# An mLSTM with two feed-forward layers on one core: q-k products in plain fp32 for eighteen more units, and two small TensorE groups joined

## The chip, the cores and the metric

The kernel runs on one core of a Trainium2 chip. The metric is the device time of one execution in microseconds, of which the median of several runs is given. TensorE is written PE, VectorE DVE, ScalarE ACT, GpSimd POOL; SP issues the transfers (DMAs).

## The reference

An mLSTM over 4 batches, 8 heads, 768 steps and head dimension 40 is followed by two feed-forward layers on its 3072 x 320 output. All is in fp32 (the weights arrive as float64).

```python
for t in range(S):                                     # mLSTM, per batch and head
    m_new = maximum(f[t] + m, i[t])
    f_stab, i_stab = exp(f[t] + m - m_new), exp(i[t] - m_new)
    C = f_stab * C + i_stab * outer(v[t], k[t])
    n = f_stab * n + i_stab * k[t]
    y[t] = sigmoid(o_gate[t]) * (C @ q[t]) / maximum(abs(n @ q[t]), 1.0)
x = y as (3072, 320)
x = ((x @ w1) * (x @ w2) @ w3) @ w_out                 # d_ff 1024
out = maximum(maximum(x @ w1b, x @ w2b), x @ w3b) @ w_outb   # d_ff 768
```

## The kernel before

**The mLSTM is done in chunks.** A sequence of 768 steps is cut into eight chunks of 88 and one of 64. A *unit* is one chunk of one batch for four heads; there are 72, and 18 make a batch. Two units (the two head groups) make one chunk of x. For unit u the kernel forms, per head, `s` = the products of 88 keys with 88 queries, `pk` = s times the decay weights `dd` (with the carried state's rows beneath), and `o` = pk against the values and a column of ones, which also yields the state of the next chunk. DVE then updates the state part of `kv` of unit u+2 and divides (four small instructions on `rd`, into `y`), POOL multiplies by the gate, PE transposes y (`xt`), and ACT and DVE split the transposed x into two parts, `xh` (rounded to the reduced form fp32r) and `xl` (the rest).

**How s is formed.** For the first `NP` = 10 units it is a plain fp32 matmul of 40 rows from tile `raw` (line 565). From unit 10 on q and k are split too: the load brings copies of q and k on 120 partitions, ACT rounds them into `qs` (line 571) and `kst` (573), POOL subtracts for qs (575) and DVE for kst (579), and one fp32r matmul over 120 rows adds the three products (line 586). The o matmuls (line 606) are fp32 throughout.

**The layers are done in token blocks of 384**, eight of them, in pairs: block A of two token blocks, then block C of the two. A group (lines 678 to 682) is eight fp32r matmuls of 384 columns into a `wk` bank. Block A has 8 steps of two groups (the product of x@w1 and x@w2); its result, split by ACT (`ph`) and POOL or DVE (`pl`), goes against w3@w_out (lines 745 to 749), a product that the kernel forms itself from fp32 matmuls, the *folds* (line 906). Block C has 6 steps of three groups (the maximum), and lines 764 for w_outb. Weights arrive as float64 and are turned into fp32 by ACT and DVE in *granules* (lines 833 to 856), then split into two parts (`wah`/`wal`, `wch`/`wcl`, 866 and 869) or stacked (`war`, `wcr`, 881 and 888).

**What sets the order.** No engine's order is written by hand. The program notes every operation with its engine, a duration in ns, and what it reads and writes; `Plan.run` then plays the whole program with these durations, with latencies between engines (`LAT`), with a clock for PE and a bus for the DMAs (`XFER`), and gives a free engine the ready operation with the least latest start, shifted by a table of biases by engine and tile (`BIAS`). The order so found is the order in which the engines' instructions are issued. `USTEPS` and `UNEXT` say behind which steps of a pair of token blocks a new unit is begun. Both s and o use the two `aq` banks of PSUM.

Of the kernel before, what the change touches and what calls it, by code (L numbers as in the profile page):

```python
# [8 lines left out]
F32 = mybir.dt.float32  # L9
# [16 lines left out]
NG = 3 * NC  # L26
NU = B * NCH * 2
GL = [L] * 8 + [64]
NP = 10
FOLDS = (3,6,9)  # L30
XLAG = 1
NPR = 7
# [6 lines left out]
L_BUFS = 4  # L39
RCP = 8  # L40
RAW0 = 3
LAST = (NBLK - 1, 1, NC - 1)
LATE = ("A", 1, 4)
BUF = dict(x=3, y=3, og=4, ph=2, ev=3, raw=2, kv=3, vs=3, qq=2, dd=4, qs=2, pk=2, rd=5)
LAT = dict(
    PA=200, PV=200, AV=130, AG=160, GA=90, GV=90, VA=130, VG=155, VP=200, AP=200, GP=230, DA=-50, DV=-50, DG=-30, DP=-50,
    VD=150, GD=150, AD=150,
)
AHEAD = 2500
GRAB = dict(V=140, G=177)  # L50
XFER = 1.45
BIAS = {"Add": -32750, "Aev": 31250, "Ag": -210500, "Akst": -383000, "Aph": -77500, "Aqs": -262250,
        "Asa": -13500, "Asg": 43250, "Astg": 57250, "Asx": 232000, "Awa": 7750, "Awar": -174000,
        "Awb": -221500, "Awc": 71000, "Awcr": -19750, "Awd": -55000, "Axh": -124000, "Dcs": -138250,
        "Ddd": 34000, "Ddna": 62500, "Dev": 75000, "Dg": -534000, "Dkv": 54250, "Dkvb": -129250, "Dqq": -96500,
        "Draw": 58250, "Dsg": -183000, "Dstg": 57750, "Dsx": -234500, "Dvs": 56750, "Gdd": 194250,
        "Gg": 144250, "Gmp": -23000, "Gpk": -77750, "Gpl": 36250, "Gqqb": -55750, "Gqs": -400500,
        "Gvsb": 10500, "Gwa": 379750, "Gwar": 219500, "Gwc": 102000, "Gwcr": 176500, "Gwd": 49000,
        "Gy": -128500, "Pac0": 27250, "Pac1": -309750, "Pac2": -91000, "Po": 7500, "Ppt": -14000, "Ps": -61250,
        "Pwk": 14250, "Pxt": -39750, "S-": -110000, "Sg": -305500, "Vam": -30000, "Vev": 474750, "Vg": -54250,  # L60
        "Vkst": 81500, "Vkv": -147750, "Vmp": -268500, "Vpk": -108500, "Vsa": -44000, "Vsg": 32250,
        "Vstg": 104500, "Vsx": -56500, "Vwb": -108500, "Vxl": 80250, "Vy": -35250, "Vzero": -14500}
TICK = 10240 / 3
WARM = 0
BANKS = ("wk", "aq", "ac0", "ac1", "ac2")
STOP = ("A", 0, 4)
U0 = (1, 1, 1, 1, 1, 1, 1, 1)
USTEPS = (8, 9, 11, 12, 15, 16, 20, 21, 23, 25, 27)
UNEXT = (0, 1, 2, 3, 4, 6, 7)


# [206 lines left out]
def mlstm_moe_kernel(  # L278
# [78 lines left out]
    def new(key, shape, dt, tag):  # L357
        P.tile(key, tag, len(slots[tag]))
        made[key] = view(slots[tag][turn[tag] % len(slots[tag])], shape, dt)
        turn[tag] += 1  # L360
        if gates_done.get(tag):
            P.state[key][0][None] = gates_done[tag]
        return key

    def T(*key):
        return made[key]

    def dma(ns, fn, r=(), w=()):
        return P.op("D", ns, fn, r, w)
# [148 lines left out]
            P.op("V", 69 + 6.25 * DM / RCP, lambda sl=sl: V.reciprocal(out=T(*t)[:, sl], in_=T(*t)[:, sl]), w=[t])  # L518

    def unit(u):  # L520
        load(u + 2)
        b, c, g, n, r = ub(u)
        h0 = b * 8 + g * 4
        if u < NP:
            new(("raw", u), [48, 4, 2 * L], F32, "raw0")
            dma(333, lambda: SP.dma_start(out=T("raw", u), in_=qk0[g, c]), w=[("raw", u)])
        else:
            new(("raw", u), [120, 2, 4, L], F32, "raw")
            dma(888, lambda: SP.dma_start(out=T("raw", u), in_=qk[b, g, c]), w=[("raw", u)])
# [30 lines left out]
        if u < NP:  # L560

            def f():
                raw = T("raw", u)
                for h in range(4):
                    PE.matmul(T("s", u)[:L, h], lhsT=raw[0:40, h, L:2 * L], rhs=raw[0:40, h, 0:n], start=True, stop=True)

            P.op("P", 720, f, r=[("raw", u)], w=[("s", u)])
        else:
            ks = kst[u % 2]
            new(("qs", u), [120, 4, n], F32R, "qs")  # L570
            P.op("A", act(4 * n), lambda: A.copy(out=T("qs", u), in_=T("raw", u)[:, 0, :, 0:n]),  # L571
                 r=[("raw", u)], w=[("qs", u)])
            P.op("A", act(4 * n), lambda: A.copy(out=ks, in_=T("raw", u)[:, 1]),
                 r=[("raw", u)], w=[("kst", u % 2, 1)])
            P.op("G", 889, lambda: G.tensor_tensor(  # L575
                out=T("qs", u)[0:40], in0=T("raw", u)[0:40, 0, :, 0:n], in1=T("qs", u)[0:40].bitcast(F32),
                op=ALU.subtract,
            ), r=[("raw", u)], w=[("qs", u)])
            P.op("V", dve(4 * n), lambda: V.tensor_tensor(
                out=ks[64:104], in0=T("raw", u)[64:104, 1], in1=ks[64:104].bitcast(F32),  # L580
                op=ALU.subtract,
            ), r=[("raw", u)], w=[("kst", u % 2, 1)], port=1)

            def f():
                for h in range(4):
                    PE.matmul(T("s", u)[0:L, h], lhsT=ks[:, h], rhs=T("qs", u)[:, h], start=True, stop=True)  # L586

            P.op("P", 390, f, cols=90, r=[("qs", u), ("kst", u % 2)], w=[("s", u)])
        if L < r:

            def scaled(e):
# [7 lines left out]
        if u < 10:
            new(("o", u), [128, 4, 41], F32, f"ac{u % 3}")  # L600
        else:
            new(("o", u), [128, 4, 41], F32, "aq")

        def f():
            for h in range(4):
                PE.matmul(T("o", u)[:m, h], lhsT=T("pk", u)[:r, h, 0:m], rhs=T("kv", u)[:r, h, 40:81],  # L606
                          start=True, stop=True)

        P.op("P", 910 if m > n else 500, f, cols=210, r=[("pk", u), ("kv", u)], w=[("o", u)])
        if m > n:  # L610
            P.op("V", dve(164), lambda: V.scalar_tensor_tensor(
                out=T("kv", u + 2)[64:128, :, 40:81], in0=T("o", u)[64:128], scalar=cs[64:128, 168:169],
                in1=T("vs", u + 2)[64:128], op0=ALU.mult, op1=ALU.add,
            ), r=[("o", u), ("kv", u + 2, "k"), ("vs", u + 2)], w=[("kv", u + 2, "s")])
# [308 lines left out]
    def late_w(q):  # L923
# [13 lines left out]
            return ()  # L937
        before = switch[-1:]
        if q == 1:
            assert cur[0] >= NP and folds[0] == NA  # L940
            for key, (_, _, acc) in P.state.items():
                if key[0] in ("raw", "sg", "w3", "wo", "sx", "mp"):
                    before += acc
# [19 lines left out]
    def more():  # L963
        u = cur[0]
        if u < NU:
            unit(u)
            if u % 2:
                pend.append(ub(u)[:2])
            cur[0] = u + 1

    folds = [0]
# [75 lines left out]
def _lay(i):  # L1047
# [77 lines left out]
```

## Time and profile before

| what | value |
| --- | --- |
| three runs | 732.37, 736.55, 738.3 us; median 736.55 |
| the profiled execution | 735.73 us |
| its span, first to last instruction | 733.9 us |
| busy: PE, DVE, ACT, POOL | 695.5, 453.4, 385.7, 337.2 us |
| mean granted clock of PE | 0.988 |
| moved by DMA | 82.48 MB |

Busy times add up the instructions of an engine; several engines work at once, so they don't add up to the span. An engine's instructions run in their order; an instruction that waits holds up those behind it. The ends of matmuls are modelled, so the distance between the starts of two matmuls is a better measure of what one costs than its own length.

### The profile page before, as it was taken

The numbers are of one execution on the slowest core, as the hardware profiler recorded it, in microseconds if no ns is written. First come the engines' busy times: TensorE is split into PE (matmuls) and PEld (weight loads), VectorE is DVE, ScalarE is ACT, GpSimd is POOL, SyncE is SP. The second block draws the span as 40 slices with busy tenths as digits, with TensorE's granted clock in tenths as the row PEclk, the third lists the DMA queues.
The fourth block names the chain that finished last, engine by engine and source line by source line (L and its number), as shares of the span: only waits on it lengthen the run. The fifth ranks groups of instructions, "written<-read, shape, count | busy, mean of one in ns | idle before, by whom it ended". The sixth has DMA issues, their size and how long they took to land.

```text
span 733.9 us, 12690 instructions
## 1 busy us (share of the span) xinstructions
PE 695.5 (95%) x4269; PEld 670.2 (91%) x4269; DVE 453.4 (62%) x1012; ACT 385.7 (53%) x728; POOL 337.2 (46%) x465
## 2 busy tenths in 40 slices
PE   1797899999999999999999999999999999999998
PEld 1675887788999999999999999999999999999998
DVE  4679998878775668475454777564454774232433
ACT  5978989888884336545334345554342342232211
POOL 1859875857744345565423555564243461000000
PEclk9999999999999999999999999999999999999999
DMA  8998777955623335433212446332222340000000
GB/s 211 251 268 244 226 217 236 239 153 161 190 88 87 102 82 148 130 92 87 75 30 70 114 102 169 94 101 80 57 68 64 92 108 1 1 0 1 1 28 27
DMA packets 52232, 82.48 MB, mean 112 GB/s; under 512 B 11864, under 2 KB 37912, under 8 KB 52168
## 3 DMA queue, kind: packets, MB, share of 16 engines
q1 hardware_dynamic: 52168, 81.69, 40.3%
q8 instruction: 33, 0.54, 0.3%
q14 instruction: 31, 0.25, 0.1%
HBM read 77.63 MB, written 4.03 MB: 111 GB/s over the span
## 4 chain that ended last, share of the span: by engine, by line
PE 78%; DMA 7%; DVE 4%; ACT 4%; POOL 3%; issue 2%; SPq 0%; POOLq 0%; DVEq 0%; ACTq 0%
PE wk L678 12%; PE wk L680 12%; PE wk L679 12%; PE ac L764 8%; PE aq L606 6%; PE wk L682 6%; PE wk L681 6%; PE ac L745 4%; PE ac L749 4%; DMA dd<-d_na 4%; PE ac L747 3%; PE aq L586 2%; PE wk L906 1%; PE aq L646 1%; ACT stg L850 1%
## 5 line engine op out<-in xcount | busy, mean ns | idle before, releaser
L698 POOL TENSOR_TENSOR pl<-pr,ph 128x384 fp32r<-128x384 f32 (+1 forms) x30 | 31.2, 1040 | 161.1 <-ACT ph L694 141.9
L694 ACT CAST ph<-pr 128x384 fp32r<-128x384 f32 (+1 forms) x114 | 57.4, 507 | 86.3 <-PE ac L764 38.3
L678 PE MATMUL wk<-xh,wch 128*128 128x384 f32 x288 | 99.6, 346 | 0.2 <-ACT pr L726 0.2
L729 DVE TENSOR_TENSOR pr<-pr,wk 128x384 f32<-128x384 f32 (+1 forms) x98 | 53.2, 545 | 71.0 <-PE wk L682 67.9
L680 PE MATMUL wk<-xl,wch 128*128 128x384 f32 x288 | 97.1, 337 | 0.0
L679 PE MATMUL wk<-xh,wcl 128*128 128x384 f32 x288 | 97.0, 337 | 0.0
L698 DVE TENSOR_TENSOR pl<-pr,ph 128x384 fp32r<-128x384 f32 (+1 forms) x84 | 53.6, 638 | 67.3 <-ACT ph L694 66.5
L678 PE MATMUL wk<-xh,wah 128*128 128x384 f32 x256 | 91.7, 358 | 1.6 <-ACT xh L657 1.6
L680 PE MATMUL wk<-xl,wah 128*128 128x384 f32 x256 | 87.5, 342 | 2.8 <-DVE xl L660 2.8
L679 PE MATMUL wk<-xh,wal 128*128 128x384 f32 x256 | 87.4, 342 | 0.8 <-DVE wal L869 0.8
L575 POOL TENSOR_TENSOR qs<-misc,qs 40x352 fp32r<-40x352 f32 (+1 forms) x62 | 66.4, 1072 | 39.8 <-ACT qs L571 37.9
L541 POOL TENSOR_TENSOR dd<-am,dd 128x352 f32<-128x352 f32 (+2 forms) x72 | 59.9, 831 | 53.8 <-DMA dd<-d_na 49.1
L726 ACT COPY pr<-wk 128x384 f32<-128x384 f32 x48 | 23.2, 484 | 89.8 <-PE wk L682 89.8
L632 POOL TENSOR_TENSOR misc<-misc 88x160 f32<-88x160 f32 (+1 forms) x62 | 42.6, 687 | 54.5 <-DVE misc L627 54.2
L711 ACT COPY pr<-wk 128x384 f32<-128x384 f32 x64 | 31.0, 484 | 68.6 <-PE wk L682 68.6
L606 PEld LDWEIGHTS aq<-kv,pk 128*128 128x128 f32 (+2 forms) x496 | 59.3, 184 | 5.0 <-issue 2.2
L713 DVE TENSOR_TENSOR pr<-pr,wk 128x384 f32<-128x384 f32 x64 | 35.4, 553 | 41.7 <-PE wk L682 40.7
L606 PE MATMUL aq<-kv,pk 128*128 128x41 f32 (+2 forms) x496 | 58.9, 268 | 1.7 <-DVE misc L627 1.4
L850 ACT ACTIVATE stg<-stg 128x512 f16<-128x512 f32 (+2 forms) x41 | 52.2, 1281 | 7.4 <-DVE stg L842 6.7
L549 ACT ACTIVATE dd<-dd 128x352 f32<-128x352 f32 (+2 forms) x72 | 35.2, 490 | 39.9 <-POOL dd L545 36.0
L678 PEld LDWEIGHTS wk<-xh,wch 128*128 128x128 f32 x288 | 54.2, 188 | 0.5 <-ACT pr L726 0.5
L679 PEld LDWEIGHTS wk<-xh,wcl 128*128 128x128 f32 x288 | 54.2, 188 | 0.0
(130 smaller groups left out, 1755.7 us busy)
## 6 DMA issues: line engine op xcount, KB each, us to landing
misc<-in_qk SPq DMA_DIRECT2D x62, 330.0 KB
dd<-d_na SPq DMA_DIRECT2D x56, 176.0 KB
kv<-in_kv SPq DMA_DIRECT2D x72, 121.5 KB
stg<-in_w3t SPq DMA_DIRECT2D x13, 512.0 KB
stg<-in_wc SPq DMA_DIRECT2D x9, 512.0 KB
qq<-in_qk SPq DMA_DIRECT2D x64, 66.0 KB
misc<-in_og SPq DMA_DIRECT2D x31, 120.0 KB
out<-misc SPq DMA_DIRECT2D x23, 160.0 KB
```

The source lines that it names most:

```text
L541: P.op("G", 735, lambda: G.tensor_tensor(out=T("dd", u)[:r], in0=am[:r, c, h0:h0 + 4].unsqueeze(2).to_broadcast([r, 4, n]), in1=T("dd", u) ...
L575: P.op("G", 889, lambda: G.tensor_tensor(out=T("qs", u)[0:40], in0=T("raw", u)[0:40, 0, :, 0:n], in1=T("qs", u)[0:40].bitcast(F32), op=ALU ...
L606: PE.matmul(T("o", u)[:m, h], lhsT=T("pk", u)[:r, h, 0:m], rhs=T("kv", u)[:r, h, 40:81], start=True, stop=True)
L678: PE.matmul(p, lhsT=h_[:, kt], rhs=xh[:, kt], start=kt == 0, stop=False)
L679: PE.matmul(p, lhsT=l_[:, kt], rhs=xh[:, kt], start=False, stop=False)
L680: PE.matmul(p, lhsT=h_[:, kt], rhs=xl[:, kt], start=False, stop=False)
L681: PE.matmul(p, lhsT=r_, rhs=xh[:, 2], start=False, stop=False)
L694: P.op("A", act(n), lambda sl=sl: A.copy(out=T("ph", key)[:, sl], in_=T(*src)[:, sl]), r=[src + part], w=[("ph", key) + part])
L698: e.tensor_tensor(out=T("pl", key)[:, sl], in0=T(*src)[:, sl], in1=T("ph", key)[:, sl].bitcast(F32), op=ALU.subtract)
L729: P.op("V", dve(sl.stop - sl.start), lambda ps=ps, sl=sl: V.tensor_tensor(out=T(*sc)[:, sl], in0=T(*sc)[:, sl], in1=T(*ps)[:, sl], op=ALU. ...
L764: PE.matmul(T(f"ac{m}", (k, 1)), lhsT=src[:, m * 128:m * 128 + 128], rhs=w[:, o:o + DM], start=first_, stop=last_,)
L850: A.activation(out=sign, in_=tl()[:, :, 1].bitcast(F32), func=AF.Copy)
```

## The change

Three things. `NP` goes from 10 to 28, so that units 10 to 27 form s by the plain fp32 matmul from a load of 48 partitions as well (`qk0` now holds all batches); `NQ` = 10 keeps the first ten in their own buffers. From unit `DUO` = 28 on, s of unit u and o of unit u-1 are one operation to the planner (1210 ns in place of 390 and 910), issued back to back; the loads of unit u+2 are noted after o of unit u-1, what followed an o before (the state's update, y, the gate) is now the function `rest`, and a chunk becomes due for its transpose when its y is done. The planner's latencies from ACT to DVE and to POOL go from 130 to 165 and from 160 to 210 ns, `XFER` from 1.45 to 1.5, one more step (26) begins a unit, and the table of biases is another.

```diff
-NP = 10
+NP = 28
+NQ = 10
+DUO = 28
-    PA=200, PV=200, AV=130, AG=160, GA=90, ...
+    PA=200, PV=200, AV=165, AG=210, GA=90, ...
-XFER = 1.45
+XFER = 1.5
-BIAS = {"Add": -32750, "Aev": 31250, "Ag": -210500, "Akst": -383000, "Aph": -77500, "Aqs": -262250,
+BIAS = {"Add": -25500, "Aev": 67500, "Ag": -141500, "Akst": -365750, "Aph": -135500, "Aqs": -321000,
...
-USTEPS = (8, 9, 11, 12, 15, 16, 20, 21, 23, 25, 27)
+USTEPS = (8, 9, 11, 12, 15, 16, 20, 21, 23, 25, 26, 27)
...
     def unit(u):
-        load(u + 2)
+        if u < DUO:
+            load(u + 2)
...
         if u < NP:
-            new(("raw", u), [48, 4, 2 * L], F32, "raw0")
-            dma(333, lambda: SP.dma_start(out=T("raw", u), in_=qk0[g, c]), w=[("raw", u)])
+            new(("raw", u), [48, 4, 2 * L], F32, "raw0" if u < NQ else "raw")
+            dma(333, lambda: SP.dma_start(out=T("raw", u), in_=qk0[b, g, c]), w=[("raw", u)])
...
+            duo = u >= DUO
+            if duo:
+                new(("o", u - 1), [128, 4, 41], F32, "aq")
+
             def f():
                 for h in range(4):
                     PE.matmul(T("s", u)[0:L, h], lhsT=ks[:, h], rhs=T("qs", u)[:, h], start=True, stop=True)
-
-            P.op("P", 390, f, cols=90, r=[("qs", u), ("kst", u % 2)], w=[("s", u)])
+                if duo:
+                    outs(u - 1)
+
+            if duo:
+                P.op("P", 1210, f, cols=300, r=[("qs", u), ("kst", u % 2), ("pk", u - 1), ("kv", u - 1)],
+                     w=[("s", u), ("o", u - 1)])
+            else:
+                P.op("P", 390, f, cols=90, r=[("qs", u), ("kst", u % 2)], w=[("s", u)])
...
-        P.op("P", 910 if m > n else 500, f, cols=210, r=[("pk", u), ("kv", u)], w=[("o", u)])
+        if u >= DUO:
+            rest(u - 1)
+            load(u + 2)
+        if u + 1 < DUO or u == NU - 1:
+            new(("o", u), [128, 4, 41], F32, f"ac{u % 3}" if u < 10 else "aq")
+            P.op("P", 910 if m > n else 500, lambda: outs(u), cols=210, r=[("pk", u), ("kv", u)], w=[("o", u)])
+            rest(u)
+
+    def outs(u):
+        b, c, g, n, r = ub(u)
+        m = 128 if c < NCH - 1 else n
+        for h in range(4):
+            PE.matmul(T("o", u)[:m, h], lhsT=T("pk", u)[:r, h, 0:m], rhs=T("kv", u)[:r, h, 40:81], start=True, stop=True)
+
+    def rest(u):
...
```

In the order of the changed program the lines are about 20 higher: 565 becomes 569, 586 becomes 594, 606 becomes 625, 646 becomes 666, 678 to 682 become 698 to 702, 694 becomes 714, 711 becomes 731.

The first place is ACT in the first block A, between the second and the third eviction of a `wk` bank (`COPY pr<-wk`). Before:

```order
L711 COPY pr_115<-wk_131 128x384
L833 ACTIVATE stg_111<-stg_111 128x512
L839 ACTIVATE sx_121<-sx_121 128x512
L866 CAST wah<-stg_113 128x512
L850 ACTIVATE stg_111<-stg_111 128x512
L573 CAST kst_74<-misc 120x352
L573 CAST kst_75<-misc 120x352
L571 CAST qs_94<-misc 120x352
L571 CAST qs_95<-misc 120x352
L694 CAST ph_87<-pr_115 128x384
L711 COPY pr_116<-wk_130 128x384
```

And now:

```order
L731 COPY pr_115<-wk_131 128x384
L870 ACTIVATE stg_111<-stg_111 128x512
L859 ACTIVATE sx_121<-sx_121 128x512
L714 CAST ph_87<-pr_115 128x384
L853 ACTIVATE sx_121<-sx_121 128x512
L886 CAST wah<-stg_111 128x512
L731 COPY pr_116<-wk_130 128x384
```

The four casts of q and k of two units are gone, and the granules of weights have moved up by one.

The second place is PE in the same block, around its third group. Before, an s, the group, and then another s with an o:

```order
L682 MATMUL wk_130<-xl_83,war 128x384
L586 MATMUL aq_133<-qs_94,kst_74 88x88 x4
L678 MATMUL wk_131<-xh_80,wah 128x384
L679 MATMUL wk_131<-xh_80,wal 128x384
L680 MATMUL wk_131<-xl_83,wah 128x384
L678 MATMUL wk_131<-xh_80,wah 128x384
L679 MATMUL wk_131<-xh_80,wal 128x384
L680 MATMUL wk_131<-xl_83,wah 128x384
L681 MATMUL wk_131<-xh_80,war 128x384
L682 MATMUL wk_131<-xl_83,war 128x384
L586 MATMUL aq_133<-qs_95,kst_75 88x88 x4
L606 MATMUL aq_132<-kv_104,pk_96 128x41 x4
```

And now:

```order
L702 MATMUL wk_130<-xl_83,war 128x384
L569 MATMUL aq_133<-misc 88x88 x4
L625 MATMUL aq_132<-kv_104,pk_96 128x41 x4
L698 MATMUL wk_131<-xh_80,wah 128x384
L699 MATMUL wk_131<-xh_80,wal 128x384
```

The s reads the loaded tile itself (`misc` holds raw), it stands ahead of the o, and the first of the two s's has moved to before the first group.

The third place is PE in the block A of token block 2, with the fp32r s of one unit. Before, it stands ahead of a transpose, and the o comes some groups later:

```order
L682 MATMUL wk_131<-xl_83,war 128x384
L586 MATMUL aq_132<-qs_94,kst_74 88x88 x4
L646 MATMUL aq_133<-cs,misc 128x88 x3
L678 MATMUL wk_129<-xh_80,wah 128x384
L679 MATMUL wk_129<-xh_80,wal 128x384
```

And now:

```order
L769 MATMUL ac_135<-pl_88,wb 128x384
L594 MATMUL aq_133<-qs_94,kst_74 88x88 x4
L625 MATMUL aq_132<-kv_104,pk_97 128x41 x4
L698 MATMUL wk_131<-xh_80,wah 128x384
L699 MATMUL wk_131<-xh_80,wal 128x384
```

The s and the o of the unit before it stand together, as in 44 places of the new order (6 before); the transpose stands elsewhere.

## Rows read from the trace of the kernel before

**Rows 1.** The page's slices: PE's busy tenths in 40 equal slices of the span.

```profile
PE   1797899999999999999999999999999999999998
```

**Rows 2.** Busy time by stage: PE, PEld, DVE, ACT, POOL, clock, DMA share, GB/s.

```profile
69.00:136.00 67.00, 58.94 (x333) 52.24 (x334) 59.57 (x117) 60.05 (x104) 49.46 (x58) 0.92 0.81 232
136.00:186.00 50.00, 47.75 (x269) 44.06 (x268) 40.11 (x86) 44.33 (x81) 35.52 (x41) 0.97 0.61 177
186.00:734.00 548.00, 543.20 (x3439) 536.31 (x3438) 306.27 (x705) 228.01 (x469) 211.37 (x297) 1.00 0.28 76
```

**Rows 3.** PE's waits from 69 to 186 us: us in total, times, longest.

```profile
PE wk L680 <- DVE xl L660: 2.8, 1, 2.8
PE aq L646 <- POOL misc L632: 1.8, 3, 0.8
PE wk L678 <- ACT xh L657: 1.6, 1, 1.6
PE aq L606 <- DVE misc L627: 1.4, 1, 1.4
PE aq L586 <- POOL pk L555: 1.1, 1, 1.1
PE wk L679 <- DVE wal L869: 0.8, 1, 0.8
PE wk L906 <- ACT qs L571: 0.6, 1, 0.6
PE aq L586 <- DVE misc L627: 0.6, 1, 0.6
```

**Rows 4.** Busy time of the three stretches at half clock, columns as in rows 2.

```profile
69.00:76.50 7.50, 4.69 (x15) 4.38 (x16) 7.25 (x11) 6.58 (x14) 7.15 (x8) 0.55 0.84 245
100.00:104.00 4.00, 4.00 (x16) 4.00 (x16) 3.77 (x11) 3.60 (x6) 3.70 (x6) 0.57 0.81 258
168.50:172.00 3.50, 3.50 (x15) 3.40 (x15) 3.10 (x5) 3.06 (x8) 2.26 (x2) 0.54 0.63 200
```

**Rows 5.** Groups by line and shape, 69 to 186 us: busy us, mean ns.

```profile
L575 POOL TENSOR_TENSOR qs<-misc,qs 40x352 fp32r<-40x352 f32 x14 | 16.9, 1213 | 4.5 <-ACT qs L571 2.9 <-PE ac L749 1.4
L579 DVE TENSOR_TENSOR kst<-misc,kst 40x352 fp32r<-40x352 f32 x16 | 14.1, 881 | 0.5
L573 ACT CAST kst<-misc 120x352 fp32r<-120x352 f32 x16 | 7.9, 503 | 0.7 <-PE aq L586 0.4 <-DMA misc<-in_qk 0.2
L571 ACT CAST qs<-misc 120x352 fp32r<-120x352 f32 x14 | 6.7, 484 | 0.0
```

**Rows 6.** PE's timeline: an fp32r s alone (start us, us).

```profile
76.86 0.44 PE L586 MATMUL aq<-qs,kst 120*88 120x88 f32 x4
77.12 0.42 PE L678 MATMUL wk<-xh,wah 128*128 128x384 f32 x1
77.39 0.34 PE L679 MATMUL wk<-xh,wal 128*128 128x384 f32 x1
77.56 0.34 PE L680 MATMUL wk<-xl,wah 128*128 128x384 f32 x1
```

**Rows 7.** PE's timeline: an fp32 s in the start-up.

```profile
57.28 0.85 PE L565 MATMUL aq<-raw 40*88 40x88 f32 x8
58.06 0.45 PE L646 MATMUL aq<-cs,misc 88*128 88x88 f32 x3
```

**Rows 8.** DMA issues of q and k from unit 10 on.

```profile
misc<-in_qk SPq DMA_DIRECT2D x62, 330.0 KB
```

**Rows 9.** PE's timeline: an o alone.

```profile
270.70 0.98 PE L606 MATMUL aq<-kv,pk 128*128 128x41 f32 x8
271.51 0.42 PE L678 MATMUL wk<-xh,wah 128*128 128x384 f32 x1
```

**Rows 10.** PE's timeline: an o directly after an s.

```profile
280.61 1.06 PE L606 MATMUL aq<-kv,pk 128*128 128x41 f32 x8
281.51 0.69 PE L764 MATMUL ac<-wd,ph 128*128 128x320 f32 x3
```

More of the change, by code (lines that the diff above doesn't have):

```diff
@@ L45 @@
 LAT = dict(
-    PA=200, PV=200, AV=130, AG=160, GA=90, GV=90, VA=130, VG=155, VP=200, AP=200, GP=230, DA=-50, DV=-50, DG=-30, DP=-50,
+    PA=200, PV=200, AV=165, AG=210, GA=90, GV=90, VA=130, VG=155, VP=200, AP=200, GP=230, DA=-50, DV=-50, DG=-30, DP=-50,
     VD=150, GD=150, AD=150,
@@ L50 @@
 GRAB = dict(V=140, G=177)
-XFER = 1.45
-BIAS = {"Add": -32750, "Aev": 31250, "Ag": -210500, "Akst": -383000, "Aph": -77500, "Aqs": -262250,
[L53 to L62, printed above, removed]
+XFER = 1.5
+BIAS = {"Add": -25500, "Aev": 67500, "Ag": -141500, "Akst": -365750, "Aph": -135500, "Aqs": -321000,
+        "Asa": -45750, "Asg": 67750, "Astg": 27000, "Asx": 241250, "Awa": -1750, "Awar": -257250,
+        "Awb": -195750, "Awc": 39750, "Awcr": -11000, "Awd": -9250, "Axh": -135750, "Dcs": -129750,
+        "Ddd": 56500, "Ddna": 63500, "Dev": 137000, "Dg": -506500, "Dkv": 54750, "Dkvb": -159000,
+        "Dqq": -44500, "Draw": 59500, "Dsg": -192750, "Dstg": 60750, "Dsx": -222250, "Dvs": 61500,
+        "Gdd": 191750, "Gg": 141750, "Gmp": -73250, "Gpk": -91000, "Gpl": 83000, "Gqqb": -72500,
+        "Gqs": -332250, "Gvsb": -42250, "Gwa": 408750, "Gwar": 289500, "Gwc": 102250, "Gwcr": 215500,
+        "Gwd": 61500, "Gy": -54000, "Pac0": 20500, "Pac1": -296000, "Pac2": -168000, "Po": -12750,
+        "Ppt": -44000, "Ps": -111500, "Pwk": 5500, "Pxt": -23250, "S-": -146000, "Sg": -268250, "Vam": -34500,
+        "Vev": 394000, "Vg": -91750, "Vkst": 65500, "Vkv": -92000, "Vmp": -289250, "Vpk": -82500,
+        "Vsa": -34250, "Vsg": 48000, "Vstg": 107750, "Vsx": -92500, "Vwb": -169000, "Vxl": 14750, "Vy": -56000,
+        "Vzero": 64250}
 TICK = 10240 / 3
@@ L598, in unit @@
         ), r=[("s", u), ("dd", u)], w=[("pk", u, 1)])
[L599 to L607, printed above, removed]
-        P.op("P", 910 if m > n else 500, f, cols=210, r=[("pk", u), ("kv", u)], w=[("o", u)])
-        if m > n:
+        if u >= DUO:
[11 more added lines that the diff above has]
+    def rest(u):
+        b, c, g, n, r = ub(u)
+        if c < NCH - 1:
             P.op("V", dve(164), lambda: V.scalar_tensor_tensor(
@@ L637, in unit @@
                  r=[("y", (b, c), 1)], w=[("y", (b, c), 2)])
+            pend.append((b, c))
     def x_cols(b, c):
@@ L939, in late_w @@
         if q == 1:
-            assert cur[0] >= NP and folds[0] == NA
+            assert cur[0] >= NQ and folds[0] == NA
             for key, (_, _, acc) in P.state.items():
@@ L966, in more @@
             unit(u)
-            if u % 2:
-                pend.append(ub(u)[:2])
             cur[0] = u + 1
@@ L1055, in _lay @@
     eye = np.eye(D, dtype=f)
-    qk0 = qk[0].transpose(0, 1, 2, 4, 3, 5)
-    qk0 = qk0.reshape(2, NCH, D, 4, 2 * L)
-    qk0 = np.concatenate([qk0, np.zeros((2, NCH, 48 - D, 4, 2 * L), f)], 2)
+    qk0 = qk.transpose(0, 1, 2, 3, 5, 4, 6)
+    qk0 = qk0.reshape(B, 2, NCH, D, 4, 2 * L)
+    qk0 = np.concatenate([qk0, np.zeros((B, 2, NCH, 48 - D, 4, 2 * L), f)], 3)
     qk = np.concatenate([qk, qk[:, :, :, 0:24], qk, qk[:, :, :, 24:40]], 3)
```

## The prediction

> **What bounds the kernel now.** I read the page's slices first. TensorE (PE) is near or over nine tenths busy in all but the first eight or nine of the 40 slices, so the kernel is a start-up followed by a long stretch that is worth exactly its matmul time [rows 1]. Then busy time by stage [rows 2]. Four stages matter: 0 to 69 us, before the first group of block A of token block 0; 69 to 136 us, that block A and the wait for token block 1; 136 to 186 us, block A of token block 1; and 186 us to the end. From 186 us PE is busy 543.20 of 548 us, at full granted clock: nothing is to be had there but fewer or cheaper matmuls, and every matmul added there is added to the end. From 69 to 186 us PE is busy 58.94 of 67 and 47.75 of 50 us, 10.3 us idle, at a mean clock of 0.92 and 0.97, while VectorE (DVE) and ScalarE (ACT) are at 60 of 67 us and GpSimd (POOL) at 49. Nobody is full, and PE waits now for one, now for another. So I asked for PE's waits in that stretch [rows 3] and for the stretches at half clock [rows 4].
>
> The waits fall in two classes. 2.8 and 1.6 us are the very start: the first group wants the two halves of x of token block 0 (xl from DVE, xh from ACT). The others, some 7.5 us as the rows add up, are holes in a running stream: transposes that wait for the gated y from POOL (1.8), an o that waits in a row of DVE work (1.4), an s that waits on POOL's queue (1.1), a weight half that DVE had not yet made (0.8), and five smaller ones. The half-clock stretches are 69 to 76.5, 100 to 104 and 168.5 to 172 us, at means of 0.55, 0.57 and 0.54, that is nearly all at 1.2 GHz, the lower of the two levels; ahead of each PE had been idle for 1 to 3 us. The second and the third cost 4.0 x 0.43 = 1.7 and 3.5 x 0.46 = 1.6 us. So 69 to 186 us holds 7.5 + 3.3 = 10.8 us that less work on DVE, ACT and POOL could give back; the start's 4.4 us and its half-clock matmuls I leave where they are.
>
> **The change part by part.** *s in fp32 for units 10 to 27.* Removed per unit: ACT copies qs (0.484 us) and kst (0.503), DVE subtracts for kst (0.881) and POOL for qs (1.213) [rows 5]. 16 of the 18 units stand between 69 and 186 us, and there these rows alone (two shorter qs left out) are 7.9 + 6.7 = 14.6 us of ACT, 14.1 of DVE and 16.9 of POOL, 14, 14 and 20% of what the engines do in that stretch (104.4, 99.7 and 85.0 us) [rows 2, 5]. None of it is on the path by itself; it is what the waits of rows 3 stand in line behind. The order shows it at its sharpest on ACT: before, four copies stand in a row between a weight's cast and the cast and eviction that block A wants next, 2 us in which ACT does nothing for PE; after, they are gone, though the planner has drawn later weight work and the x of token block 1 into part of the space.
>
> Added on PE per unit: four fp32 matmuls of 88 columns for four fp32r ones. The fp32r s takes 0.26 us from its start to the next group's start, and the first step behind it is longer by 0.1 us, 0.27 where the next is 0.17 [rows 6]. The fp32 s is there only in the start-up: eight records, 0.78 us from its start to the next start at full clock [rows 7]. In those rows it stands between other fp32 matmuls, whose weight loads are longer, so 0.78 is the upper end. The lower end is twice the fp32r one, since there are twice the records: 0.52. I take 0.61, a little over the lower end, because the record count is what the two have in common and the surroundings are not. So +0.26 to +0.52, taken as +0.35, and for 18 units **+6.3 us** (4.7 to 9.4). All of it lies on PE where PE is the bound or close to it, so it counts in full.
>
> The Trainium skill, FP8 and Floating Point Precision, section TensorE Precision Notes, says that true FP32 takes four passes through the array where the reduced form takes one. By that, an estimate from the page and the fp32r row, the s would cost 4 x 0.26 = 1.04 us, +0.78 per unit or +14.0 us in all, and the sum below would be 742. The trace does not agree, since the fp32 s as it stands in rows 7 takes 0.78 us and not 1.04.
>
> The load of raw shrinks from 330 KB a unit [rows 8] to 132 (48 x 704 values of 4 bytes), 3.6 MB in all. PE's waits of 69 to 186 us name no DMA, so this is worth nothing directly; SP issues one DMA for it as before.
>
> *s(u) and o(u-1) joined from unit 28 on.* The planner books 1210 ns for the pair where it booked 390 + 910, a saving of 90 ns in 44 groups. The rows don't show it. Alone, o takes 0.81 us to the next start [rows 9], and s 0.26, and each makes the step behind it 0.09 longer (read behind the s [rows 6], and taken for the o as well): 1.25 us. Directly after an s, o takes 0.90 [rows 10]: 0.26 + 0.90 + 0.09 = 1.25 us. The longer step between two kinds of matmul is only moved from behind the s to between s and o. So **0** us, with -4.0 (the planner's price) and +2.5 as bounds: before, 28 of the 62 fp32r s stood directly ahead of a transpose and shared that step with it, as the order of before shows, and the joined ones can't. What the join adds is a wait: o(u-1) now stands behind s(u), so it waits for qs and kst of unit u as well, and the state's update on DVE (kv of unit u+1), y and the transposes behind it. PE's order covers that: each o comes some six to twelve matmul groups earlier than before after 186 us, because a unit more is begun in each pair of blocks, and a unit comes only every few us.
>
> *Latencies and biases.* They cost nothing themselves; they move work. Between the first group and block A of token block 1 PE gets half of its folds fewer (12 of 24 fold matmuls move behind it), so that block A of block 1 can start as soon as its x is there, and the folds fill holes afterwards. For the start at 69 us the order gives no gain that I can price: the bytes ahead of the first weights are the same to within 0.2 MB, and DVE has as much work ahead of the last xl of token block 0 as before. I take 0, with 2 us either way. From 620 us on no unit is left and nothing changes.
>
> *The sum.* The profiled execution took 735.73 us (span 733.9), 0.8 below the median of the three runs, 736.55. Added +6.3. Given back: of the 10.8 us, the wait of s on POOL (1.1) and the later one of s behind DVE (0.6) go for certain, as nothing is left to wait for; of the other 9.1 I take two thirds, 6.1, because 14 to 20% of the work in front of them goes but part of the space is filled again. So 735.73 + 6.3 - 7.8 = 734.2, rounded to **734 us**, 0.3% under the median: no difference that a measurement of this kernel tells from none (about 1%, as its three runs lie 732.37 to 738.3).
>
> **The rivals.** *All holes go* (faster): the whole 10.8 comes back, the fp32 s costs its lower end, and the start is 2 us earlier: 735.7 + 4.7 - 10.8 - 2 = 728. For it: three engines lose a seventh to a fifth of their work at once, and a half-clock stretch vanishes with the hole ahead of it. Against it: DVE and ACT do as much work up to the end of the first block A as before, since later work moves up.
>
> *PE pays and the holes stay* (slower than before): one mechanism, in block A of token blocks 0 and 1. If the planner refills ACT and DVE so far that PE still waits for a weight half, a pk or a y, only the two s waits go (1.7), and at the upper price of fp32 the time is 735.7 + 9.4 - 1.7 = 743; at the price I took, 740. It decides from the point where less than 6.3 us of the 15 us of idle and half-clock time between the first group and 186 us are given back. For it: PE's own work between the first group and the first block C grows by some 6 us, to over nine tenths of that stretch.
>
> *The join pays after all*: if the planner's 90 ns are real, -4.0 us and 730. Against it stand rows 9 and 10. *The join makes PE wait*: s(u) held for POOL's qs now holds o(u-1) too; at 0.2 us for each of 44 groups, 743. Against it: in 186 us to the end PE's waits are almost nil today. *The fp32 s costs four times the fp32r one* among fp32r groups: 4 x 0.26 is 0.78 more for each of 18 units [rows 6], 735.7 + 14.0 - 7.8 = 742; rows 7 speak against it. This is the result that the page named above would give.
>
> **How the numbers follow.** Forecast 0.55; all holes go 0.17; holes stay 0.15; join pays 0.07; join waits 0.04; four times 0.02. The forecast's own bounds are some 5 us either way, from the price of fp32 (4.7 to 9.4) and the share given back. The range takes in the first two rivals: 727 to 745. Faster by over 1% is below 729.2: most of the first rival, a third of "join pays" and a tenth or more of the forecast, 0.25. Slower by over 1% is above 743.9: a little under half of the slower rivals and a small tail of the forecast, 0.14. The rest, 0.61, is within 1%.
>
> **What would show it.** In the profile of the changed kernel: the fp32 s among fp32r groups at 0.5 to 0.7 us to the next start (0.78 or more: my price is too low). PE's waits between the first group and the first block C: no s that waits for POOL, some 4 us of holes beside the start's, one half-clock stretch or none after 80 us. The first block C group starts at 184 to 188 us against 186. Joined groups: o after s at 0.90 us; 0.81 would mean that the join pays. The first group at 67 to 71 us. From the first block C to the end about 1 us longer than now, for the two units left there. The forecast is wrong if the start moves by more than 2 us, which I could not price, or if the holes of block A neither shrink nor stay but move to the folds that now lie inside it.

## The result, and the profile after

| what | before | after |
| --- | --- | --- |
| median, same chip, 8 runs each | 737.88 us (732.37 to 739.5) | 730.08 us (728.57 to 731.25) |
| ratio after / before | | 0.9913, interval 0.9888 to 0.9937 |
| profiled execution, span | 735.73, 733.9 us | 731.25, 729.3 us |

The change makes the kernel 0.9% faster, by 7.8 us in the medians. The two profiled executions are 4.5 us apart, since that of before lies 2.2 us under its median and that of after 1.2 over; what follows accounts for these 4.5 us, and the other 3.3 are the scatter of single executions.

The page's slices of after (PE's busy tenths in 40 equal slices, to hold against [rows 1]):

```profile
PE   1699999999999999999999999999999999999998
```

The fourth and fifth slices, 55 to 92 us, have filled up: from the third slice on PE is at nine tenths. Busy time by stage (PE, PEld, DVE, ACT, POOL, clock, DMA share, GB/s), the last row being the only stretch at half clock after the first group:

```profile
69.00:136.00 67.00, 63.80 (x401) 56.27 (x401) 51.27 (x124) 60.71 (x92) 44.27 (x62) 0.97 0.76 218
136.00:186.00 50.00, 50.00 (x291) 44.43 (x290) 34.46 (x79) 42.13 (x73) 27.88 (x32) 1.00 0.55 160
186.00:729.30 543.30, 539.29 (x3426) 535.09 (x3424) 303.47 (x693) 220.09 (x458) 196.47 (x279) 1.00 0.27 74
82.00:86.00 4.00, 4.00 (x16) 4.00 (x16) 3.83 (x10) 4.00 (x7) 3.84 (x5) 0.58 0.92 304
```

Against [rows 2], PE gained 4.9 and 2.3 us of busy time in the two block-A stages, and the second stage is full, at full clock. DVE lost 8.3 and 5.7 us, POOL 5.2 and 7.6; ACT lost 2.2 us in the second stage and nothing in the first, where later work has moved up. Of the three half-clock stretches in [rows 4] none stands where it stood; the one left, the last row, follows a wait of 1.4 us for POOL. PE's waits from 69 to 186 us (us in all, times, longest):

```profile
PE aq L625 <- POOL pk L559: 1.4, 1, 1.4
PE aq L569 <- DVE kv L630: 0.8, 1, 0.8
PE aq L569 <- DMA misc<-in_qk: 0.7, 1, 0.7
PE aq L569 <- DVE pk L610: 0.3, 1, 0.3
```

The eight kinds of wait shown in [rows 3], 10.7 us, have become four with 3.2. The s (line 569) now waits once for the transfer of its raw tile, and still twice behind DVE.

To compare kernels whose stages start at different times I cut the span at PE's own milestones: the first group of block A of token block 0, the first group of block C, and the last group. In each stretch the *PE work* is the number of groups of each kind times what such a group takes in the dense stream at full clock, with what it adds to the steps beside it; stretch minus PE work is the *slack*: idle time, half-clock time and steps that come late by less than the profile counts as a wait. The two kernels between these milestones (before, then after; columns as above):

```profile
68.90:186.10 117.20, 106.78 (x602) 96.40 (x602) 99.79 (x201) 104.58 (x184) 85.08 (x99) 0.94 0.72 208
186.10:723.60 537.50, 536.13 (x3394) 529.51 (x3394) 302.29 (x694) 226.70 (x465) 210.91 (x296) 1.00 0.28 76
```

```profile
71.60:184.50 112.90, 110.39 (x672) 98.01 (x671) 81.82 (x195) 99.52 (x159) 68.39 (x89) 0.98 0.67 195
184.50:719.00 534.50, 533.83 (x3391) 529.89 (x3390) 300.91 (x685) 219.63 (x457) 197.50 (x279) 1.00 0.28 74
```

| stretch | before | after | difference |
| --- | --- | --- | --- |
| to the first group | 68.9 | 71.6 | +2.7 |
| first group to first block C | 117.2 (work 98.9, slack 18.3) | 112.9 (109.0, 3.9) | -4.3: work +10.1, slack -14.4 |
| first block C to last group | 537.5 (slack 6.2) | 534.4 (2.8) | -3.1: work +0.3, slack -3.4 |
| last group to the end | 10.3 | 10.3 | 0 |

The slack can be read in the rows: from the first group to block C idle time went from 10.4 to 2.5 us, and what the lower clock costs from 6.7 us (three stretches, [rows 4]) to 1.7 (4.0 us at 0.58). The later start is no loss: before, the first group began and then stalled for 2.8 us for xl [rows 3]; after, it runs on, and the fourth group starts at 78.3 us against 79.8.

What a small group costs is read from start to start. An fp32 s between groups, a joined pair, and a transpose alone (PE's timeline of after: start, us):

```profile
86.42 0.34 PE L702 MATMUL wk<-xl,war 128*128 128x384 f32 x1
86.69 0.85 PE L569 MATMUL aq<-misc 40*88 40x88 f32 x8
87.47 0.45 PE L698 MATMUL wk<-xh,wah 128*128 128x384 f32 x1
87.76 0.33 PE L699 MATMUL wk<-xh,wal 128*128 128x384 f32 x1
...
300.32 0.39 PE L666 MATMUL aq<-cs,misc 88*128 88x88 f32 x3
300.50 0.42 PE L698 MATMUL wk<-xh,wah 128*128 128x384 f32 x1
300.76 0.34 PE L699 MATMUL wk<-xh,wal 128*128 128x384 f32 x1
...
306.00 0.44 PE L594 MATMUL aq<-qs,kst 120*88 120x88 f32 x4
306.26 1.06 PE L625 MATMUL aq<-kv,pk 128*128 128x41 f32 x8
307.15 0.42 PE L698 MATMUL wk<-xh,wah 128*128 128x384 f32 x1
307.42 0.34 PE L699 MATMUL wk<-xh,wal 128*128 128x384 f32 x1
```

The fp32 s takes 0.78 us to the next start, the step behind it 0.29 and the step ahead of it 0.27, where the dense one is 0.174: it adds 0.27 + 0.78 + 0.29 - 2 x 0.174 = 0.99 to the stream. The longer step ahead is there in all twelve places of after where an fp32 s follows a large fp32r matmul without a wait (0.26 to 0.30). Ahead of an fp32r s the step is 0.17, and the fp32r s of [rows 6] adds 0.53 - 0.174 = 0.35. So one costs **0.64** us more. The expectations below reckon with 0.90 and 0.54, which leave out the step ahead. The joined pair adds 0.26 + 0.89 + 0.27 - 0.174 = 1.25, as much as the two apart (0.35 + 0.89, medians of many). A transpose alone adds 0.18 + 0.26 - 0.174 = 0.27.

### The profile page after: what moved, and what is told of

Its sections match the earlier page's. It is cut to its first block, busy times and chain, and to the rows that moved or that the text cites. A ratio compares the mean times of both kernels' runs of the same rounds, so it can differ in the third digit from the quotient of the medians.

```text
span 729.3 us, 12666 instructions
## 1 busy us (share of the span) xinstructions
PE 699.4 (96%) x4341; PEld 674.3 (92%) x4341; DVE 437.0 (60%) x998; ACT 373.8 (51%) x697; POOL 308.3 (42%) x438
## 4 chain that ended last, share of the span: by engine, by line
PE 84%; DMA 7%; DVE 3%; POOL 2%; issue 2%; SPq 1%; ACT 0%; POOLq 0%; DVEq 0%
PE wk L698 13%; PE wk L699 12%; PE wk L700 12%; PE ac L784 9%; PE aq L625 6%; PE wk L702 6%; PE wk L701 6%; PE ac L765 4%; PE ac L769 4%; PE wk L926 4%; PE ac L767 3%; DMA stg<-in_w3t 2%; PE aq L569 2%; PE aq L594 1%; DMA dd<-d_na 1%
## 5 line engine op out<-in xcount | busy, mean ns | idle before, releaser
L718 DVE TENSOR_TENSOR pl<-pr,ph 128x384 fp32r<-128x384 f32 (+1 forms) x91 | 60.8, 669 | 75.8 <-ACT ph L714 73.1
L718 POOL TENSOR_TENSOR pl<-pr,ph 128x384 fp32r<-128x384 f32 (+1 forms) x23 | 24.2, 1052 | 153.7 <-ACT ph L714 138.9
L545 POOL TENSOR_TENSOR dd<-am,dd 128x352 f32<-128x352 f32 (+2 forms) x72 | 57.5, 799 | 49.6 <-DMA dd<-d_na 48.8
L559 POOL TENSOR_TENSOR pk<-kv,dd 128x160 f32<-128x160 f32 (+1 forms) x64 | 38.7, 606 | 72.1 <-PE aq L625 64.9
L625 PE MATMUL aq<-kv,pk 128*128 128x41 f32 (+2 forms) x496 | 62.2, 275 | 2.1 <-POOL pk L559 1.4
L625 PEld LDWEIGHTS aq<-kv,pk 128*128 128x128 f32 (+2 forms) x496 | 57.4, 184 | 4.5 <-POOL pk L559 1.7
L746 ACT COPY pr<-wk 128x384 f32<-128x384 f32 x48 | 23.1, 482 | 70.5 <-PE wk L702 70.4
L700 PEld LDWEIGHTS wk<-xl,wch 128*128 128x128 f32 x288 | 54.0, 188 | 0.0
```

The source lines that it names most:

```text
L545: P.op("G", 735, lambda: G.tensor_tensor(out=T("dd", u)[:r], in0=am[:r, c, h0:h0 + 4].unsqueeze(2).to_broadcast([r, 4, n]), in1=T("dd", u) ...
L700: PE.matmul(p, lhsT=h_[:, kt], rhs=xl[:, kt], start=False, stop=False)
L718: e.tensor_tensor(out=T("pl", key)[:, sl], in0=T(*src)[:, sl], in1=T("ph", key)[:, sl].bitcast(F32), op=ALU.subtract)
```

## The experiments

The theory: the gain is relief, that is, DVE, ACT and POOL do less between 69 and 186 us, PE's holes and its half-clock time there go, and this pays for the dearer s and more. The rivals: the gain is the new order (biases, latencies) or the join; or the shorter way from load to s, without the four instructions in between, and not the work itself.

| run | median us | ratio (interval) | first group | to block C (slack) | to last group (slack) |
| --- | --- | --- | --- | --- | --- |
| after | 730.08 | 0.9913 (0.9888 to 0.9937) | 71.6 | 112.9 (3.9) | 534.4 (2.8) |
| e1_join_tables | 745.44 | 1.0125 (1.0094 to 1.0156) | 69.7 | 126.8 (26.9) | 538.6 (8.2) |
| e2_fp32_tables | 729.14 | 0.9912 (0.9882 to 0.9942) | 71.0 | 112.1 (3.1) | 534.1 (2.5) |
| e3_tables | 742.32 | 1.0079 (1.0048 to 1.011) | 70.5 | 125.8 (25.9) | 536.1 (5.7) |
| e4_fp32 | 741.54 | 1.0078 (1.005 to 1.0107) | 70.1 | 116.7 (8.6) | 542.4 (9.9) |
| e5_old_act_latency | 734.21 | 0.9973 (0.9951 to 0.9995) | 70.0 | 116.4 (7.4) | 536.2 (4.5) |
| e6_np24 | 730.65 | 0.9921 (0.9902 to 0.9939) | 70.5 | 112.3 (4.6) | 535.4 (5.1) |
| e7_split_unread | 751.72 | 1.0209 (1.0174 to 1.0244) | 71.0 | 130.3 (21.2) | 538.1 (6.4) |
| e8_cheap_s | 728.19 | 0.9885 (0.9864 to 0.9907) | 69.2 | 110.1 (6.3) | 534.1 (3.1) |
| e9_unread_act | 738.38 | 1.001 (0.9984 to 1.0037) | 70.4 | 121.0 (12.0) | 535.1 (3.5) |
| e10_unread_dve | 744.85 | 1.0115 (1.0078 to 1.0151) | 71.5 | 130.9 (21.9) | 535.0 (3.4) |
| e11_unread_pool | 739.28 | 1.0026 (1.0005 to 1.0047) | 69.3 | 123.9 (14.9) | 534.5 (2.8) |
| e12_longer_latency | 735.67 | 0.9981 (0.9961 to 1.0002) | 69.1 | 118.2 (8.2) | 535.9 (4.2) |

Ratios are to the kernel before on the same chip; differences to after by the ratios agree with those by the medians within 1.2 us. The stretches are those of one profiled execution each.

**The parts of the change, apart.** e1 takes the fp32 s away from the changed kernel:

```diff
-NP = 28
+NP = 10
```

> The changed kernel with NP back at 10: s of units 10 to 27 from the split q and k again; the join, the biases and the latencies stay as changed. Theory, relief: the gain is holes and half-clock stretches that less ACT, DVE and POOL work gives back between the first group and the first block C, worth more than the 0.54 us that each fp32 s adds on PE (0.90 against 0.35 in the two traces); without it some 10 us of holes return and 9.7 us of PE work go, so 730 to 738 us, with PE waits over 7 us in that stretch. Rival, order: the new biases and latencies removed the holes; then the holes stay away and the 9.7 us of PE work go, 720 to 724 us. Rival, join: 730 us or less, as under the order rival, since the join is kept.

e2 takes the join away, and with it the step that begins a further unit, which goes with it:

```diff
-DUO = 28
+DUO = 72
-USTEPS = (8, 9, 11, 12, 15, 16, 20, 21, 23, 25, 26, 27)
+USTEPS = (8, 9, 11, 12, 15, 16, 20, 21, 23, 25, 27)
```

> The changed kernel without the join (DUO = 72, and without step 26 in USTEPS, which it needs): fp32 s to unit 27 and the new biases and latencies stay. Relief: 730 to 733 us, as the stretch up to the first block C is untouched; a transpose directly behind an s costs 0.07 us more than alone, some 1.5 us over 23 of them. Rival, order: the same, 730 to 733. Rival, join: back to 735 to 738 us.

e3 makes both edits, so that only biases, latencies and `XFER` are left of the change:

> The kernel before with nothing but the new biases, latencies and XFER (NP = 10, no join). Relief: about the time before or a little over, 736 to 742 us, since the biases were not made for it. Rival, order: 721 to 731 us. Rival, join: 736 to 740 us.

e4 is the kernel before with the fp32 s alone (to the changed kernel it gives the old tables, steps and latencies, and no join):

```diff
-    PA=200, PV=200, AV=165, AG=210, ...
+    PA=200, PV=200, AV=130, AG=160, ...
-XFER = 1.5
+XFER = 1.45
...
-DUO = 28
+DUO = 72
```

> The kernel before with nothing but the fp32 s for units 10 to 27 (biases, latencies, XFER and USTEPS of before, no join). Relief: 9.7 us of PE work more, and most of the 11 to 15 us of holes and half-clock stretches given back, 730 to 736 us. Rival, order: the holes stay, 743 to 748 us. Rival, join: 737 us or more.

e2 keeps all of the gain without the join, so beside the fp32 s the join is worth nothing, as its start-to-start price says. e3 and e1, slower than my theory put them, lose 0.8 and 1.25% against before: the new order without the fp32 s is bad, with some 26 us of slack ahead of block C where before has 18. But the fp32 s in the old tables loses 0.8% too (741.54 us, between what the theory and the order rival foretold). There it does what the theory says, ahead of block C (PE work 108.1, slack from 18.3 to 8.6), which just pays for the matmuls: 116.7 us against 117.2. Behind block C it loses 4.9 us, 3.7 of them new slack. So neither part is the gain alone: fp32 alone is +5.4 us, tables alone +6.1, and the two together -7. My order rival falls, and so does the plain form of the theory.

**How far the latencies matter.** e5 gives back the old ACT latencies, e12 goes on in the direction of the change:

```diff
-    PA=200, PV=200, AV=165, AG=210, ...
+    PA=200, PV=200, AV=130, AG=160, ...
```

> The changed kernel with the planner's two ACT latencies back at 130 and 160 ns; biases, XFER, fp32 s and join as changed. Relief with an order made for it: the latencies alone move few instructions, so 729 to 733 us. Rival, latencies: the planner's orders were too tight behind ACT, and the longer ones made the gain; then the holes return, 735 us or more.

```diff
-    PA=200, PV=200, AV=165, AG=210, ...
+    PA=200, PV=200, AV=200, AG=260, ...
```

> The changed kernel with the planner's ACT latencies longer once more by the same step, 200 and 260 ns. Going back to 130 and 160 cost 4.1 us. Theory, trend: the planner still books ACT's results too early, so one step more gives 726 to 729 us. Rival, fitted: the biases were found with 165 and 210, and any other order loses, 732 to 736 us.

Both lose against after, 4.1 and 5.6 us in the medians, so longer is not better by itself. A latency moves nothing on the chip; it moves the planner's choices. PE's order parts from that of after at 89 us in e5 and at 46 us in e12. The tables fit one order, and in these two runs another order of the crowded first 190 us costs some 4 to 6 us. I take that as the error bar of every run here that moves the order: e9 to e11 too.

e6 gives four of the eighteen units back to fp32r:

```diff
-NP = 28
+NP = 24
```

> The changed kernel with NP = 24: fp32 s for units 10 to 23 only, which stand before the first block C or close to it. Relief: units 24 to 27 stand where PE has few holes, so each fp32 s there costs its 0.54 us and gives nothing back: 2 us less, 727 to 729 us. Rival, order: any change of the structure under biases made for another costs more than that, 731 us or more, as the two runs that took one part alone did.

It stays at 730.65, between the two forecasts. PE's order is that of after up to 178 us, where the s of unit 24 stands, and units 24 to 27 stand where there is little to relieve. What the change gives, it gives with units 10 to 23.

**The work or the shorter chain.** e7 puts the four instructions of units 10 to 27 back into the changed kernel, into tiles that nobody reads:

```diff
+            if u >= NQ:
+                ks = kst[u % 2]
+                new(("qs", u), [120, 4, n], F32R, "qs")
+                P.op("A", act(4 * n), lambda: A.copy(out=T("qs", u)[0:48], in_=T("raw", u)[:, :, 0:n]),
+                     r=[("raw", u)], w=[("qs", u)])
...
```

> The changed kernel, with the four split instructions of units 10 to 27 put back (two on ACT, one on POOL, one on DVE, of the same sizes), but nothing reads what they write: s stays in fp32 and doesn't wait for them. Theory, relief: it is the work that counts, so the holes return, 737 to 743 us, with slack between the first group and the first block C back at 12 to 20 us. Rival, chain: it is the shorter way to s that counts (load, then matmul, with no ACT, POOL and DVE between); then the work alone costs little, 730 to 733 us.

The two copies here are of 48 partitions and not 120, but take the same 0.48 us. 751.72 us: 21.6 over the changed kernel, the worst of all and more than the theory foretold, although s waits for none of them. PE's matmuls between first group and block C are the same 672 (first row, columns as in the stages above). Its waits there (us, times, longest) name DVE alone:

```profile
71.00:201.30 130.30, 116.97 (x672) 102.81 (x671) 100.97 (x209) 109.98 (x189) 83.53 (x104) 0.93 0.58 168
```

```profile
PE aq L640 <- DVE misc L661: 4.1, 2, 2.4
PE aq L569 <- DVE pk L625: 3.8, 3, 1.6
PE aq L569 <- DVE misc L661: 3.0, 2, 2.0
PE wk L941 <- DVE wb L952: 2.5, 1, 2.5
```

Slack is 21.2 us where it was 3.9, and the clock falls to 0.93. The shorter chain falls as a cause: it is there in e7 and gives nothing. With the same tables and the long chain (e1) the stretch was even shorter, 126.8 us, with 9.2 us less PE work and 5.7 more slack. The smaller load, 132 KB in place of 330, falls as well, since e7 has it too. The work is the cause, and more so in this order, which leaves it no room.

e9, e10 and e11 put back one engine's share each, again unread: ACT's two copies, DVE's subtract, POOL's subtract (DVE's and POOL's read raw itself for both operands, so that they need no copy). Of e10:

```diff
+            if u >= NQ:
+                ks = kst[u % 2]
+                P.op("V", dve(4 * n), lambda: V.tensor_tensor(
+                    out=ks[0:40], in0=T("raw", u)[0:40, :, L:2 * L], in1=T("raw", u)[0:40, :, 0:L],
+                    op=ALU.subtract,
+                ), r=[("raw", u)], w=[("kst", u % 2, 1)], port=1)
```

> The changed kernel with only the two ACT copies of units 10 to 27 put back, read by nobody (15 us of ACT in all). All four put back cost 21.6 us. Theory, fullest engine: ACT is the fullest beside PE between the first group and the first block C (99.6 of 113 us, against 82 for DVE and 68 for POOL), so its part costs most, 8 to 15 us: 738 to 745. Rival, named engine: PE's waits with all four put back name DVE almost alone, so ACT's part costs little, 731 to 735.

> The changed kernel with only the DVE subtract of units 10 to 27 put back, read by nobody (9 to 16 us of DVE). Fullest engine: DVE has room, 31 of 113 us, so 731 to 735. Named engine: this is where most of the 21.6 us come from, 738 to 745.

> The changed kernel with only the POOL subtract of units 10 to 27 put back, read by nobody (19 us of POOL). Fullest engine: POOL has most room, 731 to 734. Named engine: nothing in PE's waits names POOL much, but POOL and DVE slow each other in such subtracts (the DVE one took 0.88 us in the crowded stretch and 0.52 as its median), so 733 to 738.

They lose 8.3, 14.8 and 9.2 us against after. The three add up to 32 where e7 lost 21.6; if 4 to 6 us of each are the order's, as e5 and e12 suggest, they come to some 17, as does e7 less the same. DVE's share is the largest by any count. Neither rule got all three: e10 lies where the named engine put it, e9 at the lower edge of what the fullest engine foretold, e11 above both. The stretch to block C and the longest waits of e10, then those of e11:

```profile
71.50:202.40 130.90, 120.76 (x673) 105.29 (x672) 97.35 (x208) 100.45 (x161) 74.01 (x90) 0.91 0.58 169
```

```profile
PE aq L569 <- DVE misc L652: 2.7, 2, 1.7
PE aq L569 <- DVE pk L616: 2.2, 1, 2.2
```

```profile
PE wk L932 <- DVE wb L943: 4.2, 1, 4.2
PE aq L569 <- DVE misc L652: 2.3, 1, 2.3
```

In e10 7.6 of the 18 us of new slack are idle time (10.1 against 2.5), the rest is clock at 0.91. And in e11, where DVE was given nothing to do, PE waits for DVE all the same: DVE is busy for 92.68 us of its longer stretch with 201 instructions, 0.46 each, where after has 81.82 with 195, 0.42 each. The Trainium skill, SBUF — State Buffer, section Who interferes with whom, says that a DVE instruction with two SBUF inputs contends with a GpSimd instruction that reads SBUF. The rows here agree with that in the main: of the commonest DVE groups those that read only SBUF got longer, and those with an operand in PSUM (aq, wk) did not. One of each, in after and then in e11:

```profile
L876 DVE SCALAR_TENSOR_TENSOR w<-stg 128x512 int32<-128x512 int32 x8 | 5.6, 696 | 5.1 <-PE wk L926 3.6 <-ACT stg L870 1.5
L610 DVE TENSOR_TENSOR pk<-aq,dd 88x352 f32<-88x352 f32 x14 | 7.2, 514 | 3.1 <-PE aq L569 3.1
```

```profile
L882 DVE SCALAR_TENSOR_TENSOR w<-stg 128x512 int32<-128x512 int32 x8 | 7.3, 907 | 7.5 <-PE wk L932 4.1 <-ACT stg L876 3.3
L616 DVE TENSOR_TENSOR pk<-aq,dd 88x352 f32<-88x352 f32 x14 | 7.2, 513 | 0.2 <-PE aq L569 0.2
```

Not all of them did (`wal<-stg,wah` went from 0.90 to 0.73 us, with three and four instructions), and no row shows that it was POOL's subtract that they waited for.

**What the fp32 s costs in place.** e8 forms s of units 10 to 27 from the tile of zeros in fp32r, so that the order on every engine stays that of after:

```diff
+                    kk, qq_ = raw[0:40, h, L:2 * L], raw[0:40, h, 0:n]
+                    if u >= NQ:
+                        kk, qq_ = zero[0:40, 0:L], zero[0:40, 0:n]
```

> The changed kernel with s of units 10 to 27 from four fp32r matmuls on a tile of zeros, in the same places and with the same costs in the plan: it leaves out the products of q and k of these units, so that only the price of fp32 on PE is taken away. Theory, PE pays in full: 18 x 0.54 = 9.7 us less, 719 to 723 us. Rival, hidden: PE would have waited there anyway for the others in the stretch before the first block C; then only part comes back, 724 to 730 us.

This takes away less than it was meant to, since these matmuls have 40 rows and not the 120 of [rows 6]:

```profile
207.15 0.34 PE L705 MATMUL wk<-xl,wcr 128*128 128x384 f32 x1
207.42 0.51 PE L572 MATMUL aq<-zero 40*88 40x88 f32 x4
207.86 0.45 PE L701 MATMUL wk<-xh,wch 128*128 128x384 f32 x1
208.14 0.34 PE L702 MATMUL wk<-xh,wcl 128*128 128x384 f32 x1
```

The s takes 0.44 us and not 0.26, with the longer steps on both sides: it adds 0.27 + 0.44 + 0.28 - 2 x 0.174 = 0.64 where the fp32 s adds 0.99. So e8 takes 0.35 us per unit from PE, 6.3 in all and 5.2 for the fifteen units between the first group and block C, and not the 9.7 of its expectation.

728.19 us, 1.9 less than after in the medians, with intervals that overlap. In the profiled execution the stretch to block C is 2.8 us shorter for 5.2 us less PE work; slack grows from 3.9 to 6.3. So about half of what the s gets cheaper there is hidden, and by the medians two thirds of the whole: a faster PE would wait more.

## Why the prediction was right, and where its sizes were off

The forecast was 734 us, 0.3% under before, in a range of 727 to 745; it came out at 730.08, 0.9% under. Direction and range hold, and so does the mechanism ahead of the first block C: work taken from three engines gives PE's holes back and pays for the dearer s. That the sum came within 4 us is in part luck. The price on PE was taken 5 us too low and what is given back 10 us too low; and with the old tables the same fp32 s (e4) is slower than before, so that the direction itself rests on the tables, to which the prediction gave nothing.

**The fp32 s**, taken as +0.35 per unit with bounds of 0.26 and 0.52, is +0.64, outside them. The choice that failed is "a little over the lower end, because the record count is what the two have in common". The 0.78 us of [rows 7] was not a matter of its surroundings: among fp32r groups it is 0.78 again, and the longer step behind it stays. The longer step ahead, 0.27 us, was not in the sum. So PE's added work is 18 x 0.64 = 11.5 us and not 6.3. The step from there to the sum, "it counts in full", failed in the other direction: of the 5.2 us that e8 takes from PE ahead of block C the stretch gives back 2.8, and of 6.3 in all the medians 1.9. The rival of four times the fp32r price is out by its mechanism, 0.78 us to the next start and not 1.04, though its price of 0.78 more lies nearer to 0.64 than mine. The Trainium skill's four passes (FP8 and Floating Point Precision, TensorE Precision Notes) are not what the step shows: 0.78 us against 0.26 is three times, in the stream 0.99 against 0.35 is 2.8, and against fp32r with the same 40 rows (e8) 0.78 against 0.44 is 1.8.

**What is given back**, taken as 7.8 of 10.8 us, is the term that was sized too small: 14.4 between first group and block C, and 3.4 behind it. I had counted the waits and two half-clock stretches; the first, behind the first group, went as well, and I had left it "where it is". The wait of s on POOL is gone, as said; that of s behind DVE is not, though "nothing is left to wait for": s waits 1.1 us there in two places. The waits left are 3.2 us against "some 4". One half-clock stretch after 80 us: right. First block C at 184.5 us against 184 to 188: right.

**From block C on** I expected 1 us more and it is 3.1 us less. PE's work there is the same within 0.3 us (two fp32 s more, four fp32r s fewer, and transposes that stand apart); the rest is slack. e2 has 2.5 us of slack without the join, and e4 with the old tables 9.9, so this is the new order's work, which I had priced at nothing from 620 us on and "PE's waits are almost nil" before it. A good part of it can be placed. Before, 23 transposes there stand directly behind an s; undisturbed such a transpose takes 0.24 us to the next start, and the 23 take 4.0 us more than that in all (22 take 4.2 more in e4, 1.4 in e2). After has no such transpose behind block C.

**The join** was right at 0: 1.25 us by both. Its upper bound of +2.5, for transposes that can no longer share the step with an s, was too high: s and transpose together add 0.59 us where neither is late and 0.69 as the median of before, apart 0.35 + 0.27 = 0.62. The rival in which the join makes PE wait would have shown behind block C, where slack is 2.8 us with the join and 2.5 without. Without the fp32 s it may be right: e1 is 3.1 us slower than e3 (their intervals overlap), with 8.2 us of slack there against 5.7.

**Latencies and biases** "cost nothing themselves; they move work", and I gave no gain to them. That step was the weakest: they are worth 12 us to the fp32 s (741.54 in e4, 729.14 in e2), and without it they cost 6. What in the table does it stays open: nearly seventy numbers were changed, and only the two latencies were tried alone. The start moved by 2.7 us against "2 us either way", which the prediction had named as a sign that it is wrong. But e8, with the same order on every engine, starts its first group at 69.2 us, 2.4 before after, so this much may be the scatter of single executions, and by the fourth group PE had made the delay up.

Of the rivals, *all holes go* came nearest: 728, by a cheap s and an earlier start that did not come, and by holes that did. *PE pays and the holes stay* is e4 in its stretch behind block C, and not after.

## What to carry to other kernels

When the busiest engine shows idle time of a few per cent with different releasers each time, look at the work of the engines that it waits for and not at the chain of any one wait: the same instructions, put back where nobody waits for them, cost over 20 us here. A dearer form on that engine can be the cheaper one for the kernel while it has holes; where PE had few, four dear units more or less made no difference that could be measured. And a planner's tables belong to the work that they were fitted to: judge an edit of the work with tables fitted anew, since old tables with new work, and new tables with old work, were both slower here.

## What the runs showed of the hardware

A small group costs more than its own time: the large matmul behind it takes 0.26 to 0.29 us to the next start where the dense step is 0.174, whatever the small one was. A fp32 s of four heads adds 0.99 us to a dense stream, a fp32r one 0.35, an o 0.89, a transpose 0.27. The step *ahead* is longer too, 0.27 us, where the s has 40 rows, in fp32 (after) and in fp32r (e8) alike; ahead of an fp32r s of 120 rows it is 0.17. Four fp32r matmuls of 40 rows take 0.44 us to the next start, four of 120 rows 0.26; whether that is the rows or e8's tile of zeros, no run tells.

A subtract of 40x352 on DVE, 0.52 us as its median over the whole span of before, took 0.88 on the mean in the crowded stretch, with POOL's subtracts there [rows 5], and 0.87 without them, in e10:

```profile
L574 DVE TENSOR_TENSOR kst<-misc 40x352 fp32r<-40x352 f32 x17 | 14.7, 868 | 0.3 <-DMA misc<-in_qk 0.2
```

So it is stretched without POOL's subtract too. Whether that adds to it no run tells: in e10 one subtract of 3.01 us lifts the mean, and the median of its 18 is 0.66, where that of the 16 in [rows 5] is 0.81.

With the new tables PE ran a part of the start-up at or near 1.2 GHz, the lower level, in all twelve kernels that have them (mean clock 0.50 to 0.68 from 45 to 58.7 us); with the old ones the clock there was 0.88 (before) and 1.00 (e4). After, and then e4:

```profile
45.00:58.70 13.70, 12.10 (x53) 10.12 (x53) 12.16 (x34) 9.63 (x15) 9.35 (x15) 0.50 0.89 246
```

```profile
45.00:58.70 13.70, 12.48 (x77) 9.61 (x76) 9.59 (x26) 11.88 (x17) 9.35 (x14) 1.00 0.94 282
```

PE gets through 53 matmul records there in place of 77, and yet the first group starts only 1.5 us later (71.6 against 70.1). Part of that would have been waiting anyway: in e4 the third matmul of the group waits 0.8 us for xl and starts at 71.7 us, in after it waits for nothing and starts at 72.2.
